# Queries and keys turned in float32 by pairs of heads, hash scores of two heads in the two halves of the array's rows, and new order tables

## The chip, the cores and the metric

The kernel runs on one core of a Trainium2 chip. The core has a matrix engine (TensorE, PE in the profile, its weight loads PEld), a vector engine (VectorE, DVE), a scalar engine (ScalarE, ACT), a general engine (GpSimd, POOL), and SyncE (SP), which here only issues DMAs. The metric is the device time of one execution in microseconds, lower is better. Before the change the median of three runs is 455.9 us (453.79, 455.90, 455.92).

## What is computed

Three layers, one behind the other, on 2 batches of 768 positions:

```python
q_bits = (einsum('bhsd,dk->bhsk', q, proj) > 0)      # 8 heads of 64, 6 hash bits each; keys likewise
mask   = q_bucket[..., :, None] == k_bucket[..., None, :]
scores = where(mask, q @ k.T / 8, -1e9)               # attention only inside a bucket
x      = softmax(scores) @ v                          # the hash attention (heads side by side: 512 wide)
# experts: causal attention for each of 4 experts with x @ wq[e], wk[e], wv[e], then @ wo[e],
# added with the gate weights of the two best experts of each position
# mix: xk, xr = blends of x with the position before it (mu_k, mu_r);
# out = sigmoid(xr @ w_r) * (relu(xk @ w_k)**2 @ w_v)
```

The results must hold float32-like accuracy, so operands are split into two float16 parts, high and low, and a product is taken as high x high + high x low + low x high.

## The kernel before

The work is cut into 12 query tiles of 128 positions (i = 0 to 11, six for each batch). For each tile there are four groups of steps: query_steps (load, split, turn, hash), lsh_steps (scores, softmax and values for 8 heads), moe_steps (the experts) and mix_steps (the last layer). key_steps prepares keys and values for four heads at a time: two groups for each batch. weight_steps splits the weights into float16 parts; the large ones arrive as 64-bit numbers and take several instructions on POOL, ACT and DVE.

Nothing is issued as the Python code runs. Every call is recorded as an operation; at the end `arrange` (L205) puts the operations in the order of a packed table (ORDER), gives each tile of the pools its buffer (HOMES) and may move a plain copy or cast to another engine (ENGINES); `issue` (L220) then emits them. All instructions therefore carry line L225, and it is names that tell them apart. Each engine works through its own queue in that order, so an instruction that waits holds up all behind it on its engine.

Names around the change, before: `k32` and `q32` are loaded keys and queries in float32, `nak` and `naq` their float16 high and low parts side by side (64 + 64 columns for a head), turned by PE against an identity (`tr_y`, `tr_x` in PSUM) and copied to `y2` and `x2` (rows of high and low part over 128 partitions). `z_k`, `z_q` are hash projections of the turned blocks against `prhl`, `zl` the part that belongs to the projection's low half. `nbk` and `nbq` hold the scaled high part once more with 12 columns of marks for the hash bits (and zeros) beside it; they are turned as well, into `y1` and `x1`. A score block of one head, `s`, is then two products for each half of the 768 keys: x1 with y1 (high x high, and the marks, which push a pair of other buckets beyond a bound) and x2 with y2 (the cross terms), each over all 128 rows of the array. `s` lies in one of two score buffers (ps_s). DVE reads it (`P<-s`, the scaled scores and their extreme), ACT takes the exponential (`P<-P`), ACT or POOL makes `PHL`'s high part, POOL its low part, a transposing DMA turns it to `PT`, and PE multiplies it with the values (`x<-v,PT`). For heads 0 and 1 of tiles 0 to 3 the turn is done by PE in float32 instead (`tp`, `PF`). The expert scores `se` take two experts at once, one in the rows 0 to 63 and one in the rows 64 to 127 of the array, and use the same two score buffers. Tiles 8 to 11 (QD) are turned by DMA.

```python
for n in range(2):                                   # L622: one head, two halves of the keys
    for a, (x, y) in enumerate((("x1", "y1"), ("x2", "y2"))):
        nc.tensor.matmul(Sp[:, n, :HS], QX[i][x][:, h, :], kg[y][:, hh, n * HS:(n + 1) * HS], ...)
```

Of the kernel before, what the change touches and what calls it, by code (L numbers as in the profile page):

```python
# [11 lines left out]
F32 = mybir.dt.float32  # L12
F16 = mybir.dt.float16
# [18 lines left out]
ST = 512.0  # L32
# [220 lines left out]
def tile_lsh_moe_mix(  # L253
# [61 lines left out]
    consts = cp.tile([P, 3 * P], F16, name="consts")  # L315
    nc.scalar.dma_start(consts, consts_in[:, :3 * P])
    ident16 = consts[:, :P]
    ident = consts[:, P:2 * P].bitcast(BF16)
    causal = consts[:, 2 * P:3 * P].bitcast(BF16)
    ident32 = cp.tile([P, P], F32, name="ident32")  # L320
    nc.gpsimd.tensor_copy(ident32, ident16)
    pr32 = cp.tile([P, NB], F32, name="pr32")
    nc.scalar.dma_start(pr32[0:64, :], proj)
    nc.scalar.dma_start(pr32[64:128, :], proj)
    prhl = cp.tile([P, 2, NB], F16, name="prhl")
    nc.vector.tensor_copy(prhl[:, 0, :], pr32)
    nc.vector.tensor_tensor(prhl[:, 1, :], pr32, prhl[:, 0, :], op=OP.subtract)
    ties = cp.tile([P, E, E], F32, name="ties")
    muk = cp.tile([P, NC], F32, name="muk")
    mur = cp.tile([P, NC], F32, name="mur")  # L330

    def late_consts():
        nc.scalar.dma_start(ties, ties_in)
        nc.gpsimd.tensor_scalar(ties, ties, -(2.0 ** -120), 1.0, op0=OP.mult, op1=OP.mult)
        nc.scalar.dma_start(muk, mu_k.rearrange("(c p) -> p c", p=P))
        nc.scalar.dma_start(mur, mu_r.rearrange("(c p) -> p c", p=P))
# [39 lines left out]
    def turn32(dst, src, n, nm, by_dma=False):  # L376

        if by_dma:
            hl = sp.tile([P, 2, n * P], F16, tag="b2", bufs=NB2, name=f"hl_{nm}")
            hi_part("a", hl[:, 0], src)  # L380
            lo_part("v", hl[:, 1], src, hl[:, 0])
# [6 lines left out]
        hi_part("a", dst[:, 0], pt)  # L388
        lo_part("v", dst[:, 1], pt, dst[:, 0])
# [82 lines left out]
    KG, KS = {}, {}  # L472

    def key_steps(b, g):
# [4 lines left out]
        def load():  # L479
            KG[b, g] = st  # L480
            st["y1"] = kp.tile([P, G, S], F16, tag="y1", name=f"y1_{nm}")
            st["y2"] = kp.tile([P, G, S], F16, tag="y2", name=f"y2_{nm}")
            st["v"] = kp.tile([P, 2, G, NT, D], F16, tag="v", name=f"v_{nm}")
            st["nb"] = []
            st["v32"] = {}

        def half(j):
            if j == 0:
                load()
            k32 = sp.tile([P, 2, NT, D], F32, tag="b3", bufs=NB3, name=f"k32_{nm}_{j}")  # L490
            LOADS.dma_start(k32, k[b, h0 + 2 * j:h0 + 2 * j + 2].rearrange(
                "h (p t) d -> p h t d", t=NT))
            na = sp.tile([P, 2, NT, P], F16, tag="b3", bufs=NB3, name=f"nak_{nm}_{j}")
            nb = sp.tile([P, 2, NT, P], F16, tag="b3", bufs=NB3, name=f"nbk_{nm}_{j}")
            st["nb"].append(nb)
            kh = na[:, :, :, D:]
            hi_part("a", kh, k32, SK)
            lo_part("v", na[:, :, :, :D], k32, kh, SK)
            hi_part("p", nb[:, :, :, :D], k32, SK)
            nc.gpsimd.memset(nb[:, :, :, D + 2 * NB:], 0.0)  # L500
            turn(st["y2"][:, 2 * j:2 * j + 2].rearrange("p h (t s) -> p (h t) s", s=P),
                 na.rearrange("p h t c -> p (h t c)"), f"y2_{nm}_{j}", (b, g) in KD, KE.get((b, g), "vv"))

        def hash_():
            z = hash_signs(lambda n: st["y2"][:, n // NT, (n % NT) * P:(n % NT + 1) * P], G * NT, f"k{nm}")
            for j in range(2):
                mark(st["nb"][j].rearrange("p h t c -> p (h t) c")[:, :, D:D + 2 * NB], z[:, j * 2 * NT:(j + 1) * 2 * NT],
                     OP.is_le, OP.is_gt)
            for j in range(2):
                turn(st["y1"][:, 2 * j:2 * j + 2].rearrange("p h (t s) -> p (h t) s", s=P),  # L510
                     st["nb"][j].rearrange("p h t c -> p (h t c)"), f"y1_{nm}_{j}", (b, g) in KD, KE.get((b, g), "vv"))
# [17 lines left out]
    NBQ = cp.tile([P, H, P], F16, name="nbq")  # L529
    nc.gpsimd.memset(NBQ[:, :, D + 2 * NB:], 0.0)  # L530

    def query_steps(i):
# [4 lines left out]
        def prep():  # L537
# [3 lines left out]
            st["na"] = na = sp.tile([P, H, P], F16, tag="b2", bufs=NB2, name=f"naq_{i}")  # L541
            nb = NBQ
# [3 lines left out]
            st["x2"] = x2 = sp.tile([P, H, P], F16, tag="b2", bufs=NB2, name=f"x2_{i}")  # L546
# [500 lines left out]
```

## Time and profile before

| | |
|---|---|
| median of three runs | 455.9 us |
| the profiled execution: time, span | 451.91 us, 450.1 us |
| PE busy | 419.1 us (93%) |
| DVE, ACT, POOL busy | 350.3, 317.9, 349.7 us (78%, 71%, 78%) |
| DMA queue of the kernel | 87.9% of 16 engines' span |
| TensorE clock granted | 1.0 in the whole span |

Busy times of PE are modelled from starts and a pipeline's length (a float16 product of 128 columns is shown with 219 ns, while the next starts about 56 ns later), so they overlap, and spacing is read from the starts. The 1.8 us between span and time lie around the span.

### The profile page before, as it was taken

How to read it: one execution, taken by the hardware profiler on the slowest of the kernel's cores; microseconds unless marked ns; L12 is line 12 of the kernel's file. 1: busy time of each engine (PE TensorE's matmuls, PEld its weight loads, DVE VectorE, ACT ScalarE, POOL GpSimd, SP SyncE). 2: the span in 40 equal slices, each digit the busy share in tenths (PEclk: the TensorE clock that was granted, in tenths of full speed). 3: DMA queues.
4: the chain of work that ended last, by engine and by line, in shares of the span. 5: the costliest groups of instructions: out<-in, count | busy, mean ns of one | idle time of the engine just before them, and what ended most of it. 6: DMA issues, size and time to landing. Idle time of an engine off the chain costs nothing.

```text
span 450.1 us, 14852 instructions
## 1 busy us (share of the span) xinstructions
PE 419.1 (93%) x5984; PEld 323.0 (72%) x5984; DVE 350.3 (78%) x900; ACT 317.9 (71%) x617; POOL 349.7 (78%) x364
## 2 busy tenths in 40 slices
PE   0776798999999999999999999999999999999996
PEld 0655686888787677885778778777678868577672
DVE  1999999999999888998878878768758765655522
ACT  2898999998988795877786666668667636662220
POOL 4898998998999786899988899978987953844020
PEclk9999999999999999999999999999999999999999
DMA  8989999999999999498899999997998885328201
GB/s 247 233 234 221 251 207 243 196 194 257 199 161 212 192 220 229 107 169 145 144 158 199 184 155 198 179 161 114 188 158 161 125 146 83 83 58 169 60 1 70
DMA packets 227157, 75.54 MB, mean 168 GB/s; under 512 B 218512, under 2 KB 222736, under 8 KB 227088
## 3 DMA queue, kind: packets, MB, share of 16 engines
q1 hardware_dynamic: 225584, 74.48, 87.9%
q8 instruction: 47, 0.77, 0.7%
q10 hardware_dynamic: 1504, 0.11, 0.2%
q14 instruction: 22, 0.18, 0.1%
HBM read 22.14 MB, written 3.15 MB: 56 GB/s over the span
## 4 chain that ended last, share of the span: by engine, by line
PE 69%; DVE 11%; POOL 3%; issue 3%; ACT 2%; DMA 1%; DVEq 0%; POOLq 0%; ACTq 0%
PE v L225 13%; PE h L225 11%; PE x L225 9%; PE s L225 9%; PE r L225 6%; PE qk L225 6%; PE o L225 4%; DVE P L225 3%; PE se L225 3%; PE vg L225 3%; PE y L225 3%; DVE v L225 2%; POOL PHL L225 1%; PE tr_y L225 1%; DMA PT<-PHL 1%
## 5 line engine op out<-in xcount | busy, mean ns | idle before, releaser
L225 POOL TENSOR_TENSOR PHL<-P,PHL 128x768 f16<-128x768 f32 x88 | 146.7, 1674 | 9.5 <-ACT PHL L225 3.6
L225 ACT ACTIVATE P<-P,mx 128x768 f32<-128x768 f32 x96 | 89.2, 931 | 20.4 <-DVE P L225 16.9
L225 DVE TENSOR_SCALAR_CACHE_REDUCE P<-s 128x768 f32<-128x768 f32 x96 | 90.7, 950 | 8.3 <-PE s L225 6.0
L225 PE MATMUL s<-y,x 128*128 128x384 f16 x384 | 76.3, 326 | 7.4 <-DVE P L225 3.7
L225 PE MATMUL h<-mk,WK 128*128 128x128 f16 x1152 | 75.0, 219 | 0.0
L225 PEld LDWEIGHTS <-WK 128*128 128x128 f16 x1152 | 67.9, 98 | 6.2 <-DVE lg L225 0.4
L225 PEld LDWEIGHTS <-PT 128*128 128x128 f16 x1584 | 54.5, 98 | 8.9 <-DMA PT<-PHL 2.2
L225 PE MATMUL x<-v,PT 128*128 128x64 f16 x1584 | 58.0, 193 | 1.9 <-DMA PT<-PHL 1.9
L225 PEld LDWEIGHTS <-x 128*128 128x128 f16 x480 | 38.0, 98 | 27.4 <-issue 7.3
L225 PE MATMUL v<-WV,k2h 128*128 128x512 f16 x192 | 57.1, 379 | 0.0
L225 POOL TENSOR_SCALAR PHL<-P 128x768 f16<-128x768 f32 x50 | 42.8, 858 | 7.3 <-ACT P L225 4.1
L225 POOL TENSOR_TENSOR PHL_m<-P_m,PHL_m 128x512 f16<-128x512 f32 (+2 forms) x24 | 33.5, 1405 | 8.9 <-ACT PHL_m L225 8.4
L225 PE MATMUL r<-WR,mr 128*128 128x512 f16 x144 | 36.0, 379 | 0.8 <-DVE k2l L225 0.8
L225 PE MATMUL qk<-xT,WQK 128*128 128x128 f16 x576 | 36.6, 219 | 0.1
L225 PE MATMUL v<-WV,k2l 128*128 128x512 f16 x96 | 36.4, 379 | 0.0
L225 ACT ACTIVATE t<-h 128x512 f32<-128x512 f32 x24 | 14.2, 594 | 28.0 <-PE h L225 27.9
L225 PEld LDWEIGHTS <-WQK 128*128 128x128 f16 x576 | 33.3, 98 | 1.0 <-DVE xT L225 0.4
L225 ACT ACTIVATE PHL<-P 128x768 f16<-128x768 f32 x38 | 31.6, 838 | 2.2 <-ACT P L225 0.9
L225 DVE SCALAR_TENSOR_TENSOR h<-h,t 128x512 f32<-128x512 f32 x24 | 16.7, 694 | 18.8 <-ACT t L225 18.7
L225 PEld LDWEIGHTS <-k2h 128*128 128x128 f16 x192 | 16.8, 98 | 13.8 <-issue 0.7
L225 ACT ACTIVATE P_m<-P_m,bias_m 128x512 f32<-128x512 f32 (+2 forms) x24 | 19.7, 821 | 8.7 <-DVE P_m L225 8.7
L225 ACT ACT_TABLE_LOAD x16 | 20.5, 1283 | 6.5 <-DMA pr<-in_proj_dram 5.0
(172 smaller groups left out, 882.9 us busy)
## 6 DMA issues: line engine op xcount, KB each, us to landing
raw_k<-in_moe_w_k_dram SPq DMA_DIRECT2D x8, 512.0 KB, 4.8
raw_v<-in_moe_w_v_dram SPq DMA_DIRECT2D x8, 512.0 KB, 4.4
k<-in_k_dram SPq DMA_DIRECT2D x8, 384.0 KB, 5.1
q<-in_q_dram SPq DMA_DIRECT2D x12, 256.0 KB, 4.7
v<-in_v_dram SPq DMA_DIRECT2D x8, 384.0 KB, 4.3
out_dram<-e SPq DMA_DIRECT2D x12, 256.0 KB, 2.6
raw_r<-in_moe_w_r_dram SPq DMA_DIRECT2D x4, 512.0 KB, 4.9
PT<-PHL SPq DMA_TRANSPOSE x88, 4.6
```

Source lines behind the costliest of these rows:

```text
L225: getattr(getattr(self.nc, engine), method)(*[real(a) for a in args], **{k: real(a) for k, a in kw.items()})
```

## The change

Keys and queries are no longer split ahead of the turn. PE turns the loaded float32 blocks (two heads of 64 columns make one block of 128, `tk` and `tr_q` in PSUM), and behind the turn ACT or DVE writes the high part (`yh`, first half of `x2`) and DVE the low part (`yl`, second half). Marks stand alone in `mkk` and `mkq` (cleared once, at the start), 12 columns for each head of a pair, and are turned into `ym` and `xm`: one float16 block for a pair of heads instead of two. `prhl` is laid out as two diagonal blocks, so that a projection handles two heads, with high and low part added up in PSUM. A score step makes two heads: marks, high x high, high x low and low x high, each over 64 rows, head 2c in the rows 0 to 63 and head 2c + 1 in the rows 64 to 127, and takes both score buffers at once. Identity, causal bound and tie breaks are no longer loaded but made on POOL (MEMSET and AFFINE_SELECT), `mu` is loaded by rows and turned on PE. The last tile's product with w_v is made and stored in two halves of 256 columns. All three tables are new, so the order changes everywhere.

```diff
+    def pattern(name, shape, dt, steps, rows, op, fill):
+        t = cp.tile(shape, dt, name=name)
+        nc.gpsimd.memset(t, 0.0)
+        nc.gpsimd.affine_select(t, t, pattern=steps, compare_op=op, fill=fill, base=0, channel_multiplier=rows)
+        return t
...
-    nc.scalar.dma_start(consts, consts_in[:, :3 * P])
+    ident16 = pattern("ident16", [P, P], F16, [[-1, P]], 1, OP.not_equal, 1.0)
     ident32 = cp.tile([P, P], F32, name="ident32")
     nc.gpsimd.tensor_copy(ident32, ident16)
...
-        for j in range(n):
-            nc.tensor.matmul(z[:, j], rows(j), prhl.rearrange("p a b -> p (a b)"), start=True, stop=True)
+        for j in range(n // 2):
+            o = z[:, 2 * j:2 * j + 2].rearrange("p r a -> p (r a)")
+            for a in range(2):
+                nc.tensor.matmul(o, rows(a, j), prhl.rearrange("p r a b -> p (r a b)"), start=(a == 0), stop=(a == 1))
...
-            hi_part("a", kh, k32, SK)
-            lo_part("v", na[:, :, :, :D], k32, kh, SK)
-            hi_part("p", nb[:, :, :, :D], k32, SK)
-            nc.gpsimd.memset(nb[:, :, :, D + 2 * NB:], 0.0)
-            turn(st["y2"][:, 2 * j:2 * j + 2].rearrange("p h (t s) -> p (h t) s", s=P),
-                 na.rearrange("p h t c -> p (h t c)"), f"y2_{nm}_{j}", (b, g) in KD, KE.get((b, g), "vv"))
+            for a in range(2):
+                pt = dps(f"tk{a}_{nm}_{j}", [P, 3, P])
+                for c in range(3):
+                    nc.tensor.transpose(pt[:, c, :], k32[:, 3 * a + c].rearrange("p h d -> p (h d)"), ident32)
+                hi, lo = (y[:, j, 3 * a * P:3 * (a + 1) * P] for y in st["y"][:2])
+                pt = pt.rearrange("p n s -> p (n s)")
+                hi_part("a", hi, pt, SK)
+                lo_part("v", lo, pt, hi, SK)
...
-            nc.scalar.activation(na[:, :, :D], q32, AF.Copy, scale=SQ)
-            nc.vector.scalar_tensor_tensor(na[:, :, D:], q32, SQ, na[:, :, :D], op0=OP.mult, op1=OP.subtract)
-            nc.gpsimd.tensor_scalar(nb[:, :, :D], q32, SQ, 1.0, op0=OP.mult, op1=OP.mult)
...
+            turn32(st["x"], q32.rearrange("p h d -> p (h d)"), H // 2, f"q_{i}", i in QD, SQ)
...
+            Sp = [ps_s.tile([P, 2, 512], F32, tag="s", name=f"s_{i}_{2 * c + r}") for r in range(2)]
             for n in range(2):
-                for a, (x, y) in enumerate((("x1", "y1"), ("x2", "y2"))):
-                    nc.tensor.matmul(Sp[:, n, :HS], QX[i][x][:, h, :], kg[y][:, hh, n * HS:(n + 1) * HS],
-                                     start=(a == 0), stop=(a == 1))
+                for j, (u, w) in enumerate(((2, 2), (0, 0), (0, 1), (1, 0))):
+                    for r in range(2):
+                        rows = slice(D * r, D * r + D)
+                        nc.tensor.matmul(Sp[r][:, n, :HS], x[u][rows, c, :], y[w][rows, cc, n * HS:(n + 1) * HS],
+                                         start=(j == 0), stop=(j == 3))
...
+        def down_half(j, f):
...
+            nc.tensor.matmul(pv_, k2[0][:, f, :], WV2[f][:, 0, js], start=(f == 0), stop=False)
...
 ORDER = """
-c-jrsg8~@F5&*!x-CJC2+qP}nwr$(CZ5wS+#6}z2DPlX#d-D^6&>jHVfC7OBg8)$=3sizwP!zI4IcNvjAR-7jXbTabB+P?oFaU}{RLB7gIiWa|hg?trazhE|4-23S{OY
+c-jTQ1E3H=6ac{I-OG0UY}>YN+qP}nwr$(CZQC{Dz@R47fI{FQJOG4-+z=Mh0YVsv1mR#X5EO#|3PUI;4ke%n<Oc?UJg^puLS85U1tC4;gA5P>GD01Q3ALakw1zfN8%j
```

At the start of DVE's queue, before: `prhl` is the projection's split, `nak` and `naq` the splits of keys and queries, `x2` and `y2` copies of turned blocks, `wd_k2` weights of the last layer.

```order
L225 CAST prhl_83<-pr32_72 128x6
L225 SCALAR_TENSOR_TENSOR nak_0_0_0_85<-k32_0_0_0_80,nak_0_0_0_85 128x12x64
L225 SCALAR_TENSOR_TENSOR naq_0_103<-q32_0_95,naq_0_103 128x8x64
L225 TENSOR_TENSOR prhl_83<-pr32_72,prhl_83 128x6
L225 COPY x2_0_136<-tr_x2_0_130 128x512
L225 SCALAR_TENSOR_TENSOR nak_0_1_0_126<-k32_0_1_0_101,nak_0_1_0_126 128x12x64
L225 SCALAR_TENSOR_TENSOR nak_0_1_1_139<-k32_0_1_1_105,nak_0_1_1_139 128x12x64
L225 COPY y2_0_1_177<-tr_y2_0_1_0_1_151 128x768
L225 SCALAR_TENSOR_TENSOR wd_k21_0_149<-raw_k21_0_120,wd_k21_0_149 128x512 x2
```

And the same place now, behind four small instructions for `prhl`: `tk` and `tr_q` are the turned blocks in PSUM, `mkk` and `mkq` the marks.

```order
L224 SCALAR_TENSOR_TENSOR yl_0_1_118<-tk1_0_1_1_106,yh_0_1_116 128x384
L224 SCALAR_TENSOR_TENSOR yl_0_1_118<-tk0_0_1_1_111,yh_0_1_116 128x384
L224 TENSOR_SCALAR yh_0_1_116<-tk1_0_1_0_121 128x384
L224 SCALAR_TENSOR_TENSOR yl_0_1_118<-tk1_0_1_0_121,yh_0_1_116 128x384
L224 SCALAR_TENSOR_TENSOR yl_0_1_118<-tk0_0_1_0_129,yh_0_1_116 128x384
L224 SCALAR_TENSOR_TENSOR x2_0_145<-tr_q_0_139,x2_0_145 128x512
L224 TENSOR_TENSOR z_k0_1_156<-z_k0_1_156,zl_k0_1_186 128x24x6
L224 TENSOR_SCALAR mkk1_147<-z_k0_1_156 128x24x6
L224 COPY zl_q0_211<-z_q0_202 128x48
L224 TENSOR_SCALAR mkk1_147<-z_k0_1_156 128x24x6
L224 TENSOR_TENSOR z_q0_202<-z_q0_202,zl_q0_211 128x8x6
L224 COPY ym_0_1_231<-tr_ym_0_1_1_217 128x768
```

The splits of keys and queries moved behind PE's turn, and the marks of the first four heads stand ahead of all weight work.

PE's queue at the first score, before: one head (7 of tile 0), a weight load ahead of each product over all 128 rows.

```order
L225 LDWEIGHTS nbk_0_1_0_118
L225 MATMUL tr_y1_0_1_0_1_347<-consts_76,nbk_0_1_0_118 128x128
L225 LDWEIGHTS x1_0_243
L225 MATMUL s_0_7_359<-y1_0_1_338,x1_0_243 128x384
L225 LDWEIGHTS x2_0_136
L225 MATMUL s_0_7_359<-y2_0_1_177,x2_0_136 128x384
```

The first score now: heads 6 and 7 in turns, each product over 64 rows.

```order
L224 MATMUL tk1_0_0_0_235<-ident32_104,k32_0_0_0_97 128x128 x3
L224 LDWEIGHTS xm_0_233
L224 MATMUL s_0_6_245<-ym_0_1_231,xm_0_233 128x384
L224 LDWEIGHTS xm_0_233
L224 MATMUL s_0_7_247<-ym_0_1_231,xm_0_233 128x384
L224 LDWEIGHTS x2_0_145
L224 MATMUL s_0_6_245<-yh_0_1_116,x2_0_145 128x384
L224 LDWEIGHTS x2_0_145
L224 MATMUL s_0_7_247<-yh_0_1_116,x2_0_145 128x384
```

A pair of heads takes 16 products in one piece where each head took 4, and other work stands between pairs, no longer between heads. In the whole queue there are 72 pieces of products over 64 rows (48 pairs of heads and 24 of the experts), where there were 24; no two of them touch.

POOL's queue at the start now (before, MEMSETs of `nbk` and `nbq` stood here and then the cast of the loaded identity):

```order
L224 MEMSET prhl_80 128x24
L224 MEMSET mkk0_82 128x1536
L224 MEMSET ident16_84 128x128
L224 MEMSET ties_89 128x16
L224 ISA
L224 AFFINE_SELECT ident16_84<-ident16_84 128x128
L224 AFFINE_SELECT ties_89<-ties_89 128x16
L224 CAST ident32_104<-ident16_84 128x128
```

The identity that PE's first turn needs is now the work of these eight rows.

## Rows read from the trace of the kernel before

**Rows 1.** The page, parts 1 and 2: busy times; busy tenths in 40 slices.

```profile
PE 419.1 (93%) x5984; PEld 323.0 (72%) x5984; DVE 350.3 (78%) x900; ACT 317.9 (71%) x617; POOL 349.7 (78%) x364
...
PE   0776798999999999999999999999999999999996
...
DVE  1999999999999888998878878768758765655522
```

**Rows 2.** Busy time by stretch (its length, then each engine; clock, DMA share, GB/s).

```profile
0.00:11.20 11.20, 0.04 (x1) 0.05 (x2) 1.16 (x3) 2.66 (x4) 4.98 (x13) 1.00 0.88 247
11.20:75.00 63.80, 50.41 (x688) 40.48 (x688) 62.44 (x140) 58.79 (x119) 58.75 (x60) 1.00 1.07 228
75.00:100.00 25.00, 24.41 (x338) 20.43 (x336) 24.64 (x67) 24.80 (x53) 24.16 (x29) 1.00 1.04 213
100.00:200.00 100.00, 99.03 (x1542) 80.55 (x1541) 92.85 (x240) 84.12 (x163) 88.32 (x92) 1.00 1.00 192
200.00:300.00 100.00, 99.16 (x1485) 75.76 (x1483) 80.57 (x226) 72.78 (x145) 87.93 (x81) 1.00 1.04 173
```

**Rows 3.** The timeline at the start: start, length, engine, instruction, idle before and releaser.

```profile
6.32 0.84 ACT L225 ACTIVATE nak<-k 128x768 f16<-128x768 f32 x1
...
7.39 0.29 POOL L225 CAST ident<-consts 128x128 f32<-128x128 f16 x1 [4.56 <-DMA consts<-in_consts_dram]
...
8.60 0.21 POOL L225 TENSOR_SCALAR ties<-ties 128x16 f32<-128x16 f32 x1 [0.91 <-DMA ties<-in_ties_dram]
...
10.04 0.37 DVE L225 CAST prhl<-pr 128x6 f16<-128x6 f32 x1 [10.04 <-DMA pr<-in_proj_dram]
...
11.16 0.82 PE L225 MATMUL tr_y<-consts,nak 128*128 128x128 f16 x6 [11.16 <-DMA w_qk<-in_moe_wk_dram]
...
23.34 0.81 PE L225 MATMUL s<-y,x 128*128 128x384 f16 x4
...
24.50 0.95 DVE L225 TENSOR_SCALAR_CACHE_REDUCE P<-s 128x768 f32<-128x768 f32 x1
```

**Rows 4.** Groups of instructions by form: count, busy us, mean ns, idle before.

```profile
L225 DVE SCALAR_TENSOR_TENSOR naq<-q,naq 128x512 f16<-128x512 f32 x12 | 14.3, 1200 | 0.0
...
L225 DVE SCALAR_TENSOR_TENSOR nak<-k,nak 128x768 f16<-128x768 f32 x8 | 8.3, 1070 | 0.2 <-ACT nak L225 0.2
...
L225 DVE COPY y<-tr_y 128x768 f16<-128x768 f16 x13 | 7.1, 550 | 0.4 <-PE tr_y L225 0.3
...
L225 DVE TENSOR_TENSOR xT<-tr_x,xT 128x512 f16<-128x512 f32 x8 | 5.5, 685 | 0.1
...
L225 DVE COPY x<-tr_x 128x512 f16<-128x512 f16 x13 | 5.3, 413 | 0.7 <-PE tr_x L225 0.7
```

**Rows 5.** The timeline of PE: runs of like products (start, length of the run).

```profile
33.83 0.82 PE L225 MATMUL tp<-ident,P 128*128 128x128 f32 x6
...
57.14 0.60 PE L225 MATMUL tr_x<-ident,x 128*128 128x128 f32 x4
...
179.33 0.83 PE L225 MATMUL tr_y<-consts,nak 128*128 128x128 f16 x12
...
182.03 1.17 PE L225 MATMUL tr_y<-consts,nak 128*128 128x128 f16 x18
```

**Rows 6.** The timeline of PE around one piece of 64-row products.

```profile
322.38 0.59 PE L225 MATMUL v<-WV,k2h 128*128 128x512 f16 x2
322.81 0.38 PE L225 MATMUL v<-WV,k2l 128*128 128x512 f16 x1
323.12 0.82 PE L225 MATMUL se<-kT,qT 64*128 64x512 f16 x6
323.87 0.51 PE L225 MATMUL h<-mk,WK 128*128 128x128 f16 x6
```

**Rows 7.** What PE waited for in the whole span: total, times, longest.

```profile
PE s L225 <- DVE P L225: 3.7, 5, 1.4
```

**Rows 8.** The chain that ended last, its end.

```profile
446.33 0.69 DVE e L225
```

More of the change, by code (lines that the diff above doesn't have):

```diff
@@ L472, in tile_lsh_moe_mix @@
     KG, KS = {}, {}
+    MKK = [cp.tile([P, G // 2 * NT, P], F16, name=f"mkk{g}") for g in range(NG)]
+    MKQ = cp.tile([P, H // 2, P], F16, name="mkq")
+    for t in [*MKK, MKQ]:
+        nc.gpsimd.memset(t, 0.0)
     def key_steps(b, g):
@@ L480, in load @@
             KG[b, g] = st
-            st["y1"] = kp.tile([P, G, S], F16, tag="y1", name=f"y1_{nm}")
-            st["y2"] = kp.tile([P, G, S], F16, tag="y2", name=f"y2_{nm}")
+            st["y"] = [kp.tile([P, G // 2, S], F16, tag=f"y{a}", name=f"y{a}_{nm}") for a in "hlm"]
             st["v"] = kp.tile([P, 2, G, NT, D], F16, tag="v", name=f"v_{nm}")
-            st["nb"] = []
             st["v32"] = {}
@@ L489, in half @@
                 load()
[L490 to L496, printed above, removed]
-            hi_part("a", kh, k32, SK)
@@ L498, in half @@
-            lo_part("v", na[:, :, :, :D], k32, kh, SK)
-            hi_part("p", nb[:, :, :, :D], k32, SK)
-            nc.gpsimd.memset(nb[:, :, :, D + 2 * NB:], 0.0)
-            turn(st["y2"][:, 2 * j:2 * j + 2].rearrange("p h (t s) -> p (h t) s", s=P),
-                 na.rearrange("p h t c -> p (h t c)"), f"y2_{nm}_{j}", (b, g) in KD, KE.get((b, g), "vv"))
-        def hash_():
[L505 to L511, printed above, removed]
+            k32 = sp.tile([P, NT, 2, D], F32, tag="b3", bufs=NB3, name=f"k32_{nm}_{j}")
@@ L513, in vals @@
+        def hash_():
+            z = hash_signs(lambda a, n: st["y"][a][:, n // NT, (n % NT) * P:(n % NT + 1) * P], G * NT, f"k{nm}")
+            mk = MKK[g]
+            mark(mk.rearrange("p n (r c) -> p (n r) c", r=2)[:, :, :2 * NB], z, OP.is_le, OP.is_gt)
+            turn(st["y"][2].rearrange("p h (t s) -> p (h t) s", s=P), mk.rearrange("p n c -> p (n c)"), f"ym_{nm}")
         def vals(j):
@@ L610, in lsh_steps, with score @@
         st = {"pt": {}}
[L612 to L616 removed]
+        def score(c):
+            need(KS[b, 2 * c // G][:3] + QS_[i])
+            if c == 0:
                 st["sm"] = sp.tile([P, H], F32, tag="sm", name=f"sm_{i}")
                 st["mx"] = sp.tile([P, H], F32, tag="mx", name=f"mx_{i}")
[L619 to L621 removed]
+            y = KG[b, 2 * c // G]["y"]
+            cc = c % (G // 2)
+            x = [QX[i]["x"][:, 0], QX[i]["x"][:, 1], QX[i]["xm"]]
+            Sp = [ps_s.tile([P, 2, 512], F32, tag="s", name=f"s_{i}_{2 * c + r}") for r in range(2)]
             for n in range(2):
[L623 to L627 removed]
+                for j, (u, w) in enumerate(((2, 2), (0, 0), (0, 1), (1, 0))):
+                    for r in range(2):
+                        rows = slice(D * r, D * r + D)
+                        nc.tensor.matmul(Sp[r][:, n, :HS], x[u][rows, c, :], y[w][rows, cc, n * HS:(n + 1) * HS],
+                                         start=(j == 0), stop=(j == 3))
+            for r in range(2):
+                h = 2 * c + r
+                st["pt"][h] = softmax(Sp[r][:, :, :HS], S, -0.125 / (SQ * SK), st["sm"][:, h:h + 1],
+                                      st["mx"][:, h:h + 1], f"{i}_{h}", MASKED, (i, h) in F32T)
         def pv(h):
@@ L660, in lsh_steps @@
         for h in range(H + LAG):
-            if h < H:
-                steps.append(lambda h=h: score(h))
+            if h < H and h % 2 == 0:
+                steps.append(lambda h=h: score(h // 2))
             if h >= LAG:
@@ L904, in gate @@
                 nc.scalar.activation(e, pr, AF.Sigmoid, scale=1.0 / (SX2 * SWR))
+        def down_half(j, f):
+            need(W)
+            js = slice(j * DM // 2, (j + 1) * DM // 2)
+            if f == 0:
+                st["pv"] = dps(f"v_{i}_{j}", [P, DM // 2])
+            pv_, k2 = st["pv"], st["k2"]
+            nc.tensor.matmul(pv_, k2[0][:, f, :], WV2[f][:, 0, js], start=(f == 0), stop=False)
+            nc.tensor.matmul(pv_, k2[0][:, f, :], WV2[f][:, 1, js], start=False, stop=False)
+            nc.tensor.matmul(pv_, k2[1][:, f, :], WV2[f][:, 0, js], start=False, stop=(f == NF - 1))
+            if f < NF - 1:
+                return
+            o = st["e"][:, js]
+            nc.vector.scalar_tensor_tensor(o, pv_, 1.0 / (ST * ST * SWV2), o, op0=OP.mult, op1=OP.mult)
+            LOADS.dma_start(out[b, s0:s0 + P, js], o)
         def down(f):
@@ L921, in mix_steps @@
                                   + [lambda c=c: gate(c) for c in range(NC)]
-                                  + [lambda f=f: hidden(f) for f in range(4, NF)] + [lambda f=f: down(f) for f in range(NF)])]
+                                  + [lambda f=f: hidden(f) for f in range(4, NF)]
+                                  + ([lambda f=f: down(f) for f in range(NF)] if i < NU - 1 else
+                                     [lambda j=j, f=f: down_half(j, f) for j in range(2) for f in range(NF)]))]
     W = weight_steps()
```

171 lines of the change are left out of this document (77 added, 94 removed).

## The prediction

> **What bounds the kernel now.** I read the page first, then the busy times by stretch, then the timeline of the first 25 us, and last PE's own timeline for spacing. PE is busy for 93% of the span and shows 9 tenths in all slices but the first four, the sixth and the last [rows 1]. The stretches say where the rest lies [rows 2]: 0.04 us of work in the first 11.2 us, 50.41 of 63.80 up to 75 us, and over 97% from there to 300. So there are two regimes. Up to 75 us PE lacks work: 11.2 us before its first product and 13.4 us between products, and more than that by spacing, since busy times of PE are modelled long. In that stretch DVE is busy 62.44 of 63.80 us (98%), ACT and POOL 92% each: the ramp is set by the elementwise engines, DVE first. From 75 us on PE sets the pace, and a microsecond more of PE is a microsecond more of time.
>
> The timeline shows how the ramp begins [rows 3]. ACT has the first key split from 6.32 us on, but DVE starts at 10.04 only, behind the projection's second DMA, PE at 11.16, the first score stands at 23.34 and DVE reads it at 24.50.
>
> **The change, part by part.** Spacing on PE first, by differences of runs of unlike length [rows 5]: a float16 turn of 128 columns takes (1.17 - 0.83) / 6 = 0.057 us, a float32 one (0.82 - 0.60) / 2 = 0.11 us.
>
> *Turns.* The kernel before makes 96 + 96 float16 turns for keys and 64 + 64 for the queries of tiles 0 to 7. Now there are 48 float32 and 48 float16 for keys, 32 and 32 for queries. In the whole: 320 x 0.057 = 18.2 us against 80 x 0.11 + 80 x 0.057 = 13.4, so 4.8 us less. Only what lies behind the ramp counts: the second batch's keys, 96 x 0.057 = 5.5 against 24 x 0.11 + 24 x 0.057 = 4.0, and tiles 5 to 7, each 16 x 0.057 = 0.91 against 4 x 0.11 + 4 x 0.057 = 0.67. That is -1.5 - 0.7 = **-2.2 us**.
>
> *Scores.* A pair of heads takes 16 products of 384 columns over half the rows instead of 8 over all. Do two halves run side by side? The experts' scores already do this [rows 6]: six products of 512 columns over 64 rows are through in 323.87 - 323.12 = 0.75 us, and one such product over 128 rows takes (322.81 - 322.38) / 2 = 0.215 us, so six in a row would take 1.29. They run two at a time, and the columns cost nothing new: 8 slots before, 8 now. But the visit has a price. The last full product starts at 322.81 and would let the next start at 323.03; the first half one starts at 323.12, 0.09 us late. Three slots of 0.215 end at 323.77; the next full product starts at 323.87, 0.10 late. So each piece of 64-row products costs about 0.19 us to enter and leave. There were 24 pieces and are 72, none touching another. 48 x 0.19 = 9.1 us, of which about 12 pairs (tiles 0, 1 and half of 2 and 3) lie in the ramp, where PE waits anyway. Behind it: 36 x 0.19 = **+6.8 us**. From below this is 0 where a pair stands at a wait, from above 9.1 where the ramp becomes PE's too.
>
> *Hash projections.* 192 products of 12 columns become 192 of 24. The nearest row is the turn of 128 columns at 0.057 us; by columns 12 more of them are 0.005 us, 1 us for all. I take 0, since they stand beside weight loads of 128 columns in both kernels, with 0 to 1 us as bounds. The turn of `mu` and the two half products of the last tile (48 of 256 columns for 24 of 512) are 0 by the same reading.
>
> *The end.* The last multiply takes 0.69 us on 512 columns [rows 8]; on 256 columns some 0.4, and half the output has left by then: **-0.3 us**.
>
> *The ramp.* Here the change takes work from the bound engine, DVE. Keys of the first batch, four halves: the low part was 1.07 us a half [rows 4], now two of 384 columns, each between 0.42 and 0.69 (the 512-column read of PSUM is 0.685), say 0.55, so 4.3 becomes 4.4; of 16 copies of turned blocks about 8 fell to DVE at 0.55 = 4.4, now 2 = 1.1; one high part moved to it, +0.55. Net -2.7. Queries of five tiles: the low part falls from 1.20 to 0.69, -2.6; of 20 copies some 8 at 0.41 = 3.3, now about 3 of half the width = 0.7; one high part +0.7. Net -4.5. DVE has some 7 us less to do ahead of the same scores. POOL loses the MEMSETs and high parts of `nbk` and `nbq`, ACT two of three splits of each query.
>
> The start moves too. What PE's first product waits for is the key itself and an identity. ACT already had the key at 6.32 [rows 3], so PE can start at about 6.4, ACT's split follows, and DVE's first real work comes at about 7 instead of 10.14: 3 us. Ahead of DVE's first read of a score its queue holds some 8.5 us of work (by the forms above) where it held 14, so that read should come near 14 to 15 us, about 10 earlier than 24.50. It doesn't move the whole ramp by 10, since weight work that stood ahead of it now stands behind. Work removed plus start gives 7 + 3 = 10 for DVE; POOL and ACT are at 92% and will be the late ones for a part, so I take **-9 us**, with -3 (the start alone) and -15 (start, work and ACT's and POOL's share, all kept) as bounds.
>
> **Sum.** -9 + 6.8 - 2.2 - 0.3 = -4.7 us on the profiled execution's 451.9 us, so 447.2. The median of the runs shown is 455.9, 4.0 above the profiled one; on it the forecast is **451.2 us**.
>
> **Rivals.**
>
> *1. Pairs wait for two score buffers (slower).* A pair needs both buffers free, where a head needed one while DVE read the other. DVE's read is 0.95 us [rows 3], say 1.0 with what belongs to it: when the second read ends late, PE stands 1.0 us longer at that pair. For it: DVE is at 93% from 100 to 200 us [rows 2], so its reads come late. Against: PE waited for such reads only 3.7 us in the whole span, five times [rows 7], nearly all in the ramp, and from 200 us on DVE is at 81% and less. Four such waits outside the ramp eat the gain; at seven the kernel is slower by over 0.5%. If one in three of the 36 pairs waits, it is 12 us: 463.2. The Trainium skill (TensorEngine Tiling (Array Packing), section Gotcha 1: PSUM Pressure) says that row tiles write to different PSUM banks, so that packing rows raises the demand for PSUM; that the trace agrees can be seen in the experts' scores, which lie in separate banks, but its price shows in no row.
>
> *2. The ramp hardly moves.* If ACT, POOL or the loads (DMA share over 1.0 from 11 to 100 us) set it, only the 3 us of the start are won: -3 + 6.8 - 2.2 - 0.3 = +1.3, that is 457.2. For it: three engines at 92% or more. Against: all three lose work there.
>
> *3. The ramp moves more.* With -15 in it, 445.2.
>
> *4. The identity is late.* It is now made on POOL, with AFFINE_SELECT, an operation that no row shows. The nearest rows: POOL's first such arithmetic, on `ties`, starts 0.91 us after the cast before it has ended and was held by its DMA [rows 3], so a first use cost at most 0.9 us; and POOL stood idle for 4.56 us up to 7.39, so there is room for eight short instructions ahead of the key. If the first use cost as much as the whole delay that would still let DVE start at 10.14, 3 us of the start are lost: 454.2. The Trainium skill (GPSIMD Engine Reference, section 2.1 Instruction dispatch) puts the first call of a freshly loaded kernel at about 6 us, with nothing visible in the profile. By it the identity would stand at about 10 us and the forecast would be the 454.2 of this rival; the trace speaks against it for the first arithmetic on POOL, and no row shows it for the select.
>
> **How the numbers follow.** Chances: forecast as worked out, 448 to 454, 0.45; rival 3 0.18; rival 4 0.10; rival 2 0.12; rival 1 0.15 (at full price, or in part at 455 to 460). A measurement of this kernel can't tell less than about 0.5% (2.3 us) from no change, so faster is below 453.6 and slower above 458.2. Faster: 0.40 of the forecast's case, rival 3, and a little of rival 4: 0.60. Same: the rest of the forecast's case, most of rivals 2 and 4: 0.22. Slower: rival 1 and the tail of rival 2: 0.18. The range goes from 443 (rival 3, with runs like the profiled one) to 460 (rival 1 in part).
>
> **What would show it.** Right: PE's first product near 6.5 us, the first score near 13 to 14, stretches of PE over 97% from about 65 us instead of 75; 72 pieces of 64-row products with about 0.19 us each at their borders, two products of a pair starting together; DVE's busy time down by 10 us or more. Wrong: gaps of about 1 us in front of scores that end with DVE's `P` behind 75 us (rival 1); PE's first product at 9 us or later, behind POOL (rival 4); a ramp that ends at 72 us or later although scores start early (rival 2); or halves that start one after the other, which would add some 60 us and would void the sum.

## The result and the profile after

The changed kernel is slower: 458.2 us in the median of 20 runs (455.2 to 460.6), beside 453.5 for the kernel before in as many. The ratio is 1.0099, with a 95% interval of 1.0079 to 1.0118. The forecast was 451.2, that is 4.7 below the 455.9 of the three runs known then; the result lies 4.7 above the kernel before. The profiled execution took 458.25 us with a span of 456.5 us, at the median of its kernel; that of the kernel before took 451.91, 1.6 below its median, so the two traces lie 6.3 apart and not 4.7.

The page's parts 1 and 2 of the changed kernel answer to [rows 1]:

```profile
PE 431.4 (95%) x6233; PEld 321.4 (70%) x6233; DVE 337.0 (74%) x888; ACT 304.6 (67%) x602; POOL 328.1 (72%) x346
...
PE   5878988998999999899999999999999999999997
...
DVE  4889986899998999798878567576767665544422
```

DVE, ACT and POOL each have 13 to 22 us less to do; for DVE 10 or more was forecast. PE is busier and begins at once, yet its row has 8s up to the seventeenth slice, where it had 9s from the eighth on. The busy times by stretch, changed kernel, answer to [rows 2] (last three numbers: granted clock, DMA share, GB/s; the share is the time of all DMA packets, added up, over the time of 16 DMA engines, and can exceed 1):

```profile
0.00:11.20 11.20, 5.74 (x50) 4.76 (x51) 4.74 (x11) 3.71 (x7) 4.70 (x15) 1.00 0.93 206
11.20:75.00 63.80, 54.87 (x720) 39.73 (x717) 57.15 (x127) 53.00 (x107) 50.41 (x45) 0.97 1.10 224
75.00:100.00 25.00, 22.10 (x302) 17.19 (x301) 20.57 (x59) 19.27 (x47) 19.05 (x28) 0.93 1.18 219
100.00:200.00 100.00, 96.13 (x1499) 74.25 (x1493) 92.60 (x238) 79.43 (x162) 86.00 (x90) 1.00 1.11 201
200.00:300.00 100.00, 99.73 (x1619) 73.66 (x1617) 73.61 (x215) 70.39 (x139) 86.84 (x84) 1.00 0.93 160
```

Here lies the surprise. Up to 75 us no elementwise engine is full any more (DVE 57.15 of 63.80, before 62.44). From 75 to 100 us PE is at 88% where it was at 98%, while DVE, ACT and POOL stand idle for 4 to 6 of 25 us. No engine that computes is full there. What rose is the DMA share: 1.18 for 1.04, and 1.11 for 1.00 in the next 100 us.

The start went nearly as forecast. Rows of the timeline, changed kernel, to hold against [rows 3]:

```profile
5.26 1.51 PE L224 MATMUL tk<-ident,k 128*128 128x128 f32 x6 [5.26 <-POOL mkq L224]
...
6.69 1.20 DVE L224 SCALAR_TENSOR_TENSOR yl<-tk,yh 128x384 f16<-128x384 f32 x2 [1.22 <-ACT yh L224]
...
14.33 0.50 PE L224 MATMUL s<-ym,xm 64*128 64x384 f16 x2
14.62 0.53 PE L224 MATMUL s<-yh,x 64*128 64x384 f16 x2
14.94 0.53 PE L224 MATMUL s<-yl,x 64*128 64x384 f16 x2
...
17.11 0.96 DVE L224 TENSOR_SCALAR_CACHE_REDUCE P<-s 128x768 f32<-128x768 f32 x1 [0.91 <-PE s L224]
```

The first product stands at 5.26 us (11.16 before), the first score at 14.33 (23.34), DVE's first read of a score at 17.11 (24.50). The read was put at 14 to 15 us; it came later because the pair's products in front of it start 0.32 us apart, twice what they take later (below). So 7 to 9 us were in hand at the first score and its read, and none of them at the end.

The pieces of 64-row products cost what the experts' scores had shown [rows 6]. PE's timeline, changed kernel, around one pair:

```profile
255.97 0.69 PE L224 MATMUL x<-v,PT 128*128 128x64 f16 x18
256.49 0.60 PE L224 MATMUL v<-WV,k2h 128*128 128x512 f16 x2
...
259.73 0.69 PE L224 MATMUL x<-v,PT 128*128 128x64 f16 x18
260.35 0.34 PE L224 MATMUL s<-ym,xm 64*128 64x384 f16 x2
260.52 0.33 PE L224 MATMUL s<-yh,x 64*128 64x384 f16 x2
...
261.34 0.33 PE L224 MATMUL s<-yl,x 64*128 64x384 f16 x2
261.50 0.32 PE L224 MATMUL s<-yh,x 64*128 64x384 f16 x2
261.75 0.44 PE L224 MATMUL tr_x<-ident,x 128*128 128x128 f32 x2
```

Each row of `s` is two products, one for each head, and the next two start 0.16 us later: halves do run side by side. The last slot would end at 261.66 and the next work starts at 261.75, 0.09 late; in front, the 18 products of `x` take 0.52 us where no change of form follows (255.97 to 256.49), here 0.62, 0.10 late.

Waits for transfers, and PE's for score buffers, changed kernel, whole span (total, times, longest):

```profile
POOL raw_k L224 <- DMA raw_k<-in_moe_w_k_dram: 8.6, 2, 7.8
...
PE s L224 <- DVE P L224: 4.5, 9, 1.7
...
DVE P L224 <- DMA PT<-PHL: 3.6, 2, 3.0
...
POOL w_v L224 <- DMA w_v<-in_moe_wv_dram: 2.6, 1, 2.6
...
PE x L224 <- DMA PT<-PHL: 2.6, 4, 1.2
```

The second row answers to [rows 7] (3.7 us before): these waits grew by 0.8 us, where rival 1 had 12. In the first, POOL stood still from 5.25 to 13.10 us until the first weights had landed. The last three are 8.8 us of waits for transposed `PT` and for weights. In the kernel before, the only such wait over 1 us of a computing engine between 11.2 and 110 us was PE's:

```profile
PE x L225 <- DMA PT<-PHL: 1.9, 1, 1.9
```

The end: in the chain of waits, the last multiply is

```profile
453.24 0.42 DVE e L224
```

0.42 us, where 0.4 was forecast for 0.69 [rows 8].

### The profile page after: what moved, and what is told of

It is laid out like the page before. It is cut to its first block, busy times and chain, and to the rows that moved or that the text cites. A ratio compares the mean times of both kernels' runs of the same rounds, so it can differ in the third digit from the quotient of the medians.

```text
span 456.5 us, 15325 instructions
## 1 busy us (share of the span) xinstructions
PE 431.4 (95%) x6233; PEld 321.4 (70%) x6233; DVE 337.0 (74%) x888; ACT 304.6 (67%) x602; POOL 328.1 (72%) x346
## 5 line engine op out<-in xcount | busy, mean ns | idle before, releaser
L224 PE MATMUL h<-mk,WK 128*128 128x128 f16 x1152 | 73.3, 219 | 0.0
L224 PEld LDWEIGHTS <-WK 128*128 128x128 f16 x1152 | 66.2, 98 | 6.0 <-issue 3.2
L224 PE MATMUL s<-yh,x 64*128 64x384 f16 x384 | 66.7, 335 | 0.0
L224 PE MATMUL v<-WV,k2h 128*128 128x512 f16 (+1 forms) x208 | 57.7, 363 | 0.0
L224 PEld LDWEIGHTS <-x 64*128 64x128 f16 (+1 forms) x672 | 34.6, 97 | 22.6 <-issue 7.0
L224 POOL TENSOR_SCALAR PHL<-P 128x768 f16<-128x768 f32 x43 | 35.6, 831 | 15.3 <-ACT P L224 7.5
L224 PE MATMUL s<-ym,xm 64*128 64x384 f16 x192 | 36.8, 337 | 5.3 <-DVE P L224 4.5
L224 ACT ACTIVATE PHL<-P 128x768 f16<-128x768 f32 x45 | 37.5, 835 | 6.1 <-PE y L224 2.5
L224 PE MATMUL v<-WV,k2l 128*128 128x512 f16 (+1 forms) x104 | 37.7, 363 | 0.0
L224 PE MATMUL s<-yl,x 64*128 64x384 f16 x192 | 35.3, 335 | 0.0
```

The lines of the kernel that those rows point to most:

```text
L224: getattr(getattr(self.nc, engine), method)(*[real(a) for a in args], **{k: real(a) for k, a in kw.items()})
```

## The experiments

Theory A: entering and leaving 64-row products is what the change pays. Theory B: a pair stands at two score buffers. Theory C: TensorE's clock falls behind stalls and holds the ramp. Theory D: transfers hold the ramp of the changed kernel, so that work taken from VectorE (DVE) buys nothing; its rival E: transfers are hidden. All times are medians, each beside runs of the kernel before on the same chip. These came to 453.5 us beside the changed kernel and to 452.8 to 453.4 beside the runs, so a difference in us between rows of different sets holds to about 0.7; the ratios are free of that.

| run | us | ratio to before, 95% |
|---|---|---|
| changed kernel | 458.2 | 1.0099 (1.0079 to 1.0118) |
| e1 full rows | 451.3 | 0.9955 (0.9933 to 0.9977) |
| e2 full rows, by head | 451.1 | 0.9948 (0.9932 to 0.9963) |
| e3 before, halves | 463.6 | 1.0229 (1.0209 to 1.0250) |
| e4 before, early projection | 452.7 | 0.9990 (0.9975 to 1.0005) |
| e5 changed, half loads | 452.0 | 0.9979 (0.9956 to 1.0002) |
| e6 before, half loads | 454.5 | 1.0031 (1.0020 to 1.0043) |
| e7 full rows, half loads | 445.7 | 0.9840 (0.9820 to 0.9859) |
| e8 changed, warm start | 457.9 | 1.0113 (1.0088 to 1.0138) |
| e9 before, early start | 450.1 | 0.9947 (0.9927 to 0.9967) |
| e10 changed, long runs | 455.2 | 1.0052 (1.0033 to 1.0071) |
| e11 before, short runs | 452.1 | 0.9995 (0.9979 to 1.0011) |
| e12 before, early start, split end | 450.7 | 0.9955 (0.9939 to 0.9970) |
| e13 full rows, long runs | 450.4 | 0.9951 (0.9931 to 0.9972) |

**What the 64-row pieces cost (e1 to e3).** The edit of e1, in the changed kernel:

```diff
-                for j, (u, w) in enumerate(((2, 2), (0, 0), (0, 1), (1, 0))):
+                for j in range(2):
                     for r in range(2):
-                        rows = slice(D * r, D * r + D)
-                        nc.tensor.matmul(Sp[r][:, n, :HS], x[u][rows, c, :], y[w][rows, cc, n * HS:(n + 1) * HS],
-                                         start=(j == 0), stop=(j == 3))
+                        u, w = ((2, 2), ((0, 0), (0, 1), (1, 0), (0, 0))[2 * n + r])[j]
+                        nc.tensor.matmul(Sp[r][:, n, :HS], x[u][:, c, :], y[w][:, cc, n * HS:(n + 1) * HS],
+                                         start=(j == 0), stop=(j == 1))
```

> The changed kernel with every score pair as 8 products over all 128 rows instead of 16 over 64 rows, both heads still made together and both score buffers still taken at once; the same columns, order and buffers. It leaves out the separation of the two heads and two of the terms. The kernel has 24 pieces of 64-row products left instead of 72. Theory A (entering and leaving the 64-row form, about 0.19 us a piece, is what the changed kernel pays): 48 x 0.19 = 9.1 us less, or at least the 36 pieces behind the ramp, 6.8 us; 458.2 becomes 449 to 451.5. Theory B (a pair stands at two score buffers): nothing of that goes, 458 to within 1.5 us. Theory C (the granted clock falls after stalls in the ramp): stalls stay, so at most 1 us less than now.

451.3, that is 7.0 us less: theory A at the size of its lower bound. e2 puts the loop over `r` outside, so that the first head's four products come first:

> As the run with full rows, but head by head: the four products of the first head stand ahead of the four of the second, so the first head needs its own score buffer only and its scores stand some 0.65 us earlier for VectorE. It leaves out the same terms. The distance to the run with full rows is what taking both buffers at once costs. Theory B: another 3 to 6 us less (the waits of PE for VectorE's P, 4.5 us in the changed kernel, and VectorE's own waits for s shrink), 444 to 448. Theory A alone: within 1 us of the run with full rows. Theory C: the dips of the granted clock at 25 and 80 us go if the stalls before them were waits for the second buffer, 3 us.

451.1, the same as e1. PE's waits for DVE's `P` fell from 4.0 us in e1 to 1.0, and the time didn't move: taking both score buffers at once costs nothing that can be measured. e3, in the kernel before:

```diff
-            for n in range(2):
-                for a, (x, y) in enumerate((("x1", "y1"), ("x2", "y2"))):
-                    nc.tensor.matmul(Sp[:, n, :HS], QX[i][x][:, h, :], kg[y][:, hh, n * HS:(n + 1) * HS],
-                                     start=(a == 0), stop=(a == 1))
+            for j, (x, y) in enumerate((("x1", "y1"), ("x2", "y2"), ("x1", "y1"), ("x2", "y2"))):
+                for n in range(2):
+                    rows = slice(D * n, D * n + D)
+                    nc.tensor.matmul(Sp[:, n, :HS], QX[i][x][rows, h, :], kg[y][rows, hh, n * HS:(n + 1) * HS],
+                                     start=(j == 0), stop=(j == 3))
```

> The kernel before, with each head's 4 products over 128 rows made as 8 products over 64 rows, two side by side into the two banks of the head's score buffer; order, buffers and all other engines' work unchanged. It leaves out half of the terms and counts the others twice. It adds 96 pieces of 64-row products (one for each head) and nothing else. Theory A: 96 x 0.19 = 18.2 us if all lay on the path; less the 16 or so heads of the ramp, where PE waits anyway, 15 us: 453.5 becomes 468 to 472. Theory B or C alone (64-row products cost nothing by themselves): 453 to 455. If two halves don't run side by side, 96 x 4 x 0.16 = 61 us more.

463.6, 10.3 us more, less than the 468 to 472 of theory A. The trace has 104 such pieces for 24 and not 120, since some heads stand next to each other. By the starts of PE's products each border costs 0.09 to 0.10 us, so 80 new pieces are 15 us, and 5.8 us of that were taken from waits that PE had anyway (by spacing 24.4 us of waits in the kernel before, 18.6 here), which leaves 9 for the 10.3 measured. The price of a piece holds; what reaches the end depends on the slack where it stands.

**Whether the ramp of the kernel before follows DVE's start (e4).**

```diff
+        first = [o for o in self.order if o.eng == "ACT" and o.calls[0][1] == "dma_start"]
+        proj = [o for o in first if any("pr32" in t.kw["name"] for t in o.uses)]
+        ident = [o for o in first if any("consts" == t.kw["name"] for t in o.uses)]
+        front = proj + ident
+        self.order = front + [o for o in self.order if o not in front]
```

> The kernel before with three DMA starts put first in ScalarE's queue (the two of the projection, then the identity), nothing else moved. VectorE's first instruction waited for the second of them until 10.04 us. If the ramp is set by VectorE, as the prediction has it, its first work comes about 3 us earlier and the time falls by 2 to 3 us: 450.5 to 451.5. If another wait stands right behind (the weights' DMA that PE's first product ended with at 11.16, ScalarE's split), the start moves and the time does not: 452.5 to 454.

452.7, no difference that can be told. Its trace shows why: DVE began at 5.54 us, but POOL's queue stood still. POOL's timeline, e4:

```profile
7.15 0.94 POOL L230 CAST ident<-consts 128x128 f32<-128x128 f16 x1 [4.32 <-DMA consts<-in_consts_dram]
10.38 0.21 POOL L230 TENSOR_SCALAR ties<-ties 128x16 f32<-128x16 f32 x1 [2.29 <-DMA ties<-in_ties_dram]
10.67 0.83 POOL L230 TENSOR_SCALAR nbk<-k 128x768 f16<-128x768 f32 x1
```

A 128 x 16 operation, used from about 70 us on, waited for its transfer and held the keys' high parts behind it, and ACT's next split, which started at 11.53, waited for those. e9 and e12 below take that up.

**Whether transfers hold the ramp of the changed kernel (e5 to e7).** The edit, the same in each:

```diff
-        raw = sp.tile([P, n, 2], U32, tag="b4", bufs=NB4, name=f"raw_{nm}")
-        LOADS.dma_start(raw.rearrange("p n a -> p (n a)"), src.bitcast(U32))
+        raw = sp.tile([P, n // 2, 2], U32, tag="b4", bufs=NB4, name=f"raw_{nm}")
+        LOADS.dma_start(raw.rearrange("p n a -> p (n a)"), src.bitcast(U32)[:, :n])
...
+        top, low = (t.unsqueeze(1).to_broadcast([P, 2, n // 2]) for t in (top, low))
```

POOL's scaling of the half is made twice, so that it stays as long.

> The changed kernel with the 20 loads of 64-bit weights (512 KB each) cut to their first half; all engines still make as many elements, reading the half twice. It leaves out half of the weights of the last layer. About 13 of these loads lie before 110 us, so some 3.3 of the 24 MB moved until then are gone. Theory D (the ramp of the changed kernel is held by the DMA engines, whose share is over 1.0 from 4 to 110 us, so the work taken from VectorE and the earlier start can't be turned into time): 458.2 becomes 449 to 453, waits of PE, VectorE and POOL for PT and for loads between 40 and 175 us shrink. Theory E (VectorE's and PE's own chain holds the ramp, transfers are hidden): 457 to 458.5.

452.0: 6.2 us less.

> The same cut of the 20 weight loads in the kernel before. It leaves out half of the weights of the last layer. VectorE is busy for 98% of the ramp there, and only one wait for a transfer of 1.9 us showed on PE behind the start. Theory D: a gain of at most 2 us (451.5 to 453.4), clearly less than in the changed kernel. If the DMA engines hold the ramp of both kernels equally, the gain is the same in both.

454.5: no gain, 1.5 us more (POOL's doubled operation raises it from 58.75 to 60.53 us of the ramp). So it isn't that less data is always less time. POOL's extra work may hide a gain of its own size here; the comparison of e7 with the uncut kernel before, below, is free of that.

> Both edits in the changed kernel: score pairs over all 128 rows (separation of the heads and two terms left out) and weight loads cut to half (half of the last layer's weights left out). With full rows alone the time was 451.3, and waits of PE grew to 33.5 us by spacing, 17.8 of them between 40 and 175 us. Theory D: here the ramp's gain that was forecast appears, 451.3 becomes 443 to 446. Theory E: 450 to 451.5.

445.7: 5.6 less than e1, and 6.3 less than e5, which keeps the 64-row pieces. The waits for PT that end at PE, DVE and ACT, in e1:

```profile
PE x L224 <- DMA PT<-PHL: 6.1, 5, 2.2
...
DVE P L224 <- DMA PT<-PHL: 4.1, 4, 1.6
...
ACT PHL L224 <- DMA PT<-PHL: 2.1, 2, 1.9
```

In e7 PE's is 0.7 us in all, ACT's 0.4, and DVE's is gone. (The profiled execution of e1 took 453.7, 2.4 above its median; e2's, at 451.9, shows 4.2, 2.1 and 0.3.) The stretch from 75 us, e7, to hold against PE's 20.73 and DVE's 21.37 of 25 in e1 (22.91 and 23.54 in e2):

```profile
75.00:100.00 25.00, 22.43 (x288) 18.07 (x286) 24.52 (x68) 22.40 (x52) 23.17 (x34) 1.00 1.13 202
```

DVE is full again here. From 11.2 to 75 us it is busy for 58.63 of 63.80 us, little more than the 57.22 of e1, so this reading is of the later stretch alone. Theory D: once transfers give way, most of the forecast gain appears. e7 lies 8.8 us below e6, the kernel before under the same cut.

**Whether the clock at the start holds the ramp (e8).**

```diff
+        tc.nc.vector.memset(warm, 0.0)
+        for _ in range(10):
+            tc.nc.tensor.matmul(wps, warm[:, :P], warm, start=True, stop=True)
         nc.issue()
```

> The changed kernel, computing the same, with ten idle products of 512 columns on a cleared buffer ahead of everything on PE, which fill it from about 1 to 5 us. By spacing, PE's products run at half pace up to 18.3 us in the changed kernel. Theory C (the clock's low level at the start delays the ramp): full pace comes some 4 us earlier, the first score at 12.5 to 13.5 us instead of 14.3, and the time falls by 1 to 3 us. If the ramp is held by transfers behind it (theory D): the first score comes earlier but the time stays within 1 us of 458.2.

457.9, within 1 us: the first score came at 14.01 instead of 14.33. PE's first products did run at full pace (six turns from 5.30 us took 0.85 us, where the changed kernel's took 1.51), but PE then waited for keys and marks as before, and the granted clock fell, to 0.61 between 12 and 20 us: the pairs of the first score again start 0.32 us apart. So full pace ahead of the first score is worth nothing here; a first score at full pace was not tried.

**How much of the transfers' load the change made itself (e10, e11, e13).** The change reads keys in another order; e10 takes that back:

```diff
-            LOADS.dma_start(k32, k[b, h0 + 2 * j:h0 + 2 * j + 2].rearrange("h (p t) d -> p t h d", t=NT))
+            LOADS.dma_start(k32, k[b, h0 + 2 * j:h0 + 2 * j + 2].rearrange("h (p t) d -> p h t d", t=NT))
```

> The changed kernel with its 8 loads of keys in runs of 1536 B, as the kernel before has them, instead of runs of 256 B; the keys' order inside a block is left wrong by that. The change had turned 2048 packets of 1536 B into 12288 of 256 B: the trace of the changed kernel has 10240 more packets of 256 B than before. At 25 ns of one DMA engine for a short packet (348.5 us x 16 / 221184) and 79 ns for a long one (10.1 x 16 / 2048) that is 18.9 against 10.0 us of all 16 engines, half of it in the first 20 us. Theory D1 (these short packets are the new load on the DMA engines): 458.2 becomes 454 to 456. Theory D2 (the DMA engines are full anyway, the change only brought work up to them): 457 to 458.5.

455.2, 3.0 us less (2.5 when each is held against its own runs of the kernel before): D1. The packets in the page's part 2, the changed kernel and then e10:

```profile
DMA packets 234167, 74.95 MB, mean 164 GB/s; under 512 B 227560, under 2 KB 229872, under 8 KB 234096
```

```profile
DMA packets 223927, 74.95 MB, mean 165 GB/s; under 512 B 215272, under 2 KB 219632, under 8 KB 223856
```

The same bytes in 10240 packets less. The Trainium skill (DMA: Bandwidth & Descriptors, section Specifications) says that transfers reach line rate from 512 B on; the trace fits it, 25 ns for 256 B and 79 ns for 1536 B, so a byte in the short packets took nearly twice as long.

> The opposite edit in the kernel before: its 8 loads of keys in runs of 256 B (the keys' order is left wrong by that), all else the same. D1: the start waits for the keys, 453.2 becomes 455 to 457. D2, or transfers hidden behind VectorE's 98%: 453 to 454.

452.1, no difference, where D1 had 455 to 457: the kernel before has room for the short packets, and D1 holds for the changed kernel alone.

> The changed kernel with both measured costs taken out: score pairs over all 128 rows (separation of the heads and two terms left out) and keys loaded in runs of 1536 B (their order inside a block left wrong). Alone the first gave 458.2 to 451.3, the second 458.2 to 455.2. If they add up: 448 to 449, that is 4 to 5 us below the kernel before, about half of the 11.5 forecast for ramp, turns and end together; what is left of the DMA load (halved weight loads gave 5.6 with full rows) holds the rest. If the short packets only cost time because pairs in 64-row form came late: 451.

450.4, neither the 448 to 449 of a plain sum nor quite the 451. Beside full rows the long runs give 0.9 us, which the intervals of e1 and e13 don't tell from nothing: the two costs don't add up, and the cut weight loads show that more than the short packets is in the way.

**A version that beats both (e12, e9).** The kernel before, with e4's edit and POOL's scaling of `ties` moved back; e12 also divides the last product.

```diff
+        late = [o for o in self.order if o.eng == "POOL" and any("ties" == t.kw["name"] for t in o.uses)][:1]
+        self.order = [o for o in self.order if o not in late]
...
+        at = min(at, 300)
+        self.order[at:at] = late
```

> A candidate that beats both: the kernel before, computing the same, with the projection and the identity first in ScalarE's DMA queue, POOL's scaling of the tie breaks (it held POOL for 2.3 us in the run with the early projection, and behind it ScalarE for 4.1) moved back to before 300 operations, and the last product with w_v made in two halves of 256 columns with two stores. The end gives 0.7 us (end of the changed kernel 3.56 us by spacing, 4.24 before). If VectorE's chain holds the ramp of before, the start gives 2 to 3 more: 450 to 451. If the start is hidden as with the early projection alone: 452 to 452.5.

> The start of the faster version alone, computing the same: projection and identity first in ScalarE's DMA queue, POOL's scaling of the tie breaks moved back to before 300 operations, the end undivided. The version with the divided end came to 450.7, the early projection alone to 452.7 beside 453.4. If the end gave 0.7 of it, this gives 451.3 to 451.5; if POOL's held queue was all that kept the early start from paying, 450.7 to 451.2; if the end gave all, 452.5 to 453.

e12 450.7, e9 450.1: the start gives the whole, the divided end nothing that can be measured. POOL's and DVE's timelines, e9:

```profile
7.12 1.63 POOL L235 TENSOR_SCALAR nbk<-k 128x768 f16<-128x768 f32 x1
...
21.21 0.95 DVE L235 TENSOR_SCALAR_CACHE_REDUCE P<-s 128x768 f32<-128x768 f32 x1
```

`nbk` starts at 7.12 instead of 10.67 in e4. DVE reads its first score at 21.21, 3.3 us earlier than before [rows 3], and the time falls by 2.7, 0.5%: in the kernel before, a microsecond at the first score is nearly a microsecond at the end. DVE's first instruction alone, 4.5 us earlier in e4, was worth nothing that can be told.

## Why the prediction was wrong, step by step

- **Two regimes, the ramp set by the elementwise engines, DVE first: right for the kernel before.** e9's 3.3 us at DVE's first score came out as 2.7; e9 also freed POOL's queue, so that it was DVE rather than all three is not shown. (A slip without effect on the sum: PE's row shows less than 9 tenths in the first five slices, the seventh and the last, not in "the first four, the sixth and the last" [rows 1].)
- **Scores, +6.8: right.** Measured 7.0 (e1), 6.3 with half loads (e7 and e5) and 4.8 with long runs (e13 and e10). 48 pieces at 0.19 us are 9.1 of PE's time; the rest didn't reach the end, and that it was just the 12 pairs of the ramp, as forecast, is not shown.
- **Hash projections 0, turns -2.2, end -0.3: not contradicted, not each measured.** Together they are inside the rest below. PE's time for turns and projections fell by 4.6 us by spacing, where 4.8 was worked out for the turns; the divided end was worth nothing measurable in e12.
- **The ramp, -9: this step failed.** With the pieces taken out (e1) the kernel is 2.1 us faster than before, where -9 - 2.2 - 0.3 = -11.5 was forecast. So the ramp gave about nothing (+0.4, if turns and end gave what was worked out), and the whole miss of 9.4 us lies here. The work taken from DVE was real, and so was the early start. But the step asked only which compute engine would be late next ("POOL and ACT ... will be the late ones for a part"), and it was none of them: transfers were (DMA share 1.10 and 1.18). The share before, 1.07 and 1.04, stood in the rows [rows 2]; DVE at 98% hid it. With the weight loads halved in both kernels the same comparison gives -8.8 (-7.3 against the uncut kernel before): most of the 11.5 is there when transfers let it through, and some 3 to 4 us of the forecast would have been too much in any case.
- **Rival 2 named it and was thrown out for a wrong reason**: "Against: all three lose work there". Whichever three are meant, the loads didn't lose work. They gained 10240 packets by the keys' new order, a line of the diff that the working never priced; taken back it is worth 2.5 to 3.0 us (e10). Its sign came too: PE was at 88% from 75 to 100 us although scores began early. Its price, +1.3, was too low, since it kept the 3 us of the start, and those were lost as well.
- **Rival 1 fell** (e2: nothing). That 458.2 lies within the stated 443 to 460 is luck: the upper end stood for this rival. **Rival 3 fell** with the ramp. **Rival 4 fell**: POOL's AFFINE_SELECT for the identity took 0.29 us from 2.38 us on and the cast behind it ended at 3.33; PE's first product at 5.26 us waited for the MEMSETs of `mkk` and `mkq` behind them.
- **What was to show it**: first product, first score, 72 pieces, pairs side by side and DVE's 13 us less all came. DVE's first read of a score came 2 us late. "Stretches of PE over 97% from about 65 us" didn't: 96% from 100 to 200 us.

What stays open: how the transfers' hold divides between short packets, weight loads and the order in which SP issues them, since e10's 3.0 us shrank to 0.9 in e13; how much of it is the new order, since all tables changed and no run puts the old work in a new order; and what the dips of the clock cost by themselves (below).

## What to carry to other kernels

An engine at 98% hides what stands close behind it: before work is taken from the bound engine, list every resource of that stretch with its share, the DMA engines among them, and take the gain only down to the next one. Price each new access pattern in a diff by packets as well as bytes. And look for short operations in an in-order queue that wait for transfers nobody needs yet: here, moving one of 0.2 us and three DMA starts gave 2.7 us, where the whole change cost 4.7.

## What the runs showed of the hardware

Going into products over 64 rows and out of them costs PE 0.09 to 0.10 us each way, in 72 pieces of the changed kernel and 104 of e3 alike. The Trainium skill (TensorEngine Tiling (Array Packing), section Key Properties) says that a change of the tiling form drains TensorE, without a price; the trace fits it and gives the price.

At the start PE runs at half pace, though the profile shows a clock of 1.00 there: in the changed kernel the products of the first score start 0.32 us apart and those at 260 us 0.16; in the kernel before the first six turns took 0.82 us [rows 3], as long as twelve at 179 us [rows 5]. So the "1.0 in the whole span" of the table above doesn't hold for the start.

Later the granted clock fell behind waits of PE. Stretches with the two dips, changed kernel, and PE's timeline around the second:

```profile
24.00:28.00 4.00, 2.96 (x29) 1.82 (x28) 3.59 (x8) 3.39 (x8) 3.51 (x3) 0.64 1.01 195
...
76.00:80.00 4.00, 1.79 (x15) 1.37 (x16) 2.18 (x5) 1.15 (x3) 1.48 (x3) 0.97 0.98 208
80.00:84.00 4.00, 4.00 (x49) 2.66 (x46) 2.81 (x8) 2.77 (x6) 3.83 (x5) 0.61 1.15 247
```

```profile
78.84 0.32 PE L224 MATMUL s<-ym,xm 64*128 64x384 f16 x1 [1.66 <-DVE P L224]
79.72 0.47 PE L224 MATMUL s<-ym,xm 64*128 64x384 f16 x1 [0.56 <-DVE P L224]
79.72 0.79 PE L224 MATMUL s<-yh,x 64*128 64x384 f16 x2
80.02 0.81 PE L224 MATMUL s<-yl,x 64*128 64x384 f16 x2
80.34 0.81 PE L224 MATMUL s<-yh,x 64*128 64x384 f16 x2
```

PE was busy for 1.79 of 4 us, and then its slots took 0.32 us instead of 0.16: the level of 1.2 GHz instead of 2.4. Together the two dips cost some 3 us of PE (an estimate from these rows: 0.36 and 0.39 of 4 us each). They are not the changed kernel's own: the profiled execution of the kernel before shows none in the ramp, but e4 and e6, made from it, do (0.59 from 40 to 44 us, 0.57 from 20 to 24), and e7's ramp has none. Over the 20 runs of the changed kernel the mean clock went from 0.980 to 0.996 and hardly went with the time (correlation -0.21). It looks like a consequence of the stalls rather than a cause; no run takes it away alone.
